# Result blocks of an up stage written to DRAM by GpSimd on its own queue, one tick after they are made, instead of by SyncE two to four ticks after

## The chip, the cores and the metric

One NeuronCore of a Trainium2 chip runs the whole program. The metric is the device time of one execution in microseconds, over several runs; a profiled execution gives the trace. PE is TensorE, DVE is VectorE, ACT is ScalarE, POOL is GpSimd and SP is SyncE, which here only issues transfers.

## The reference

Attention over 4 batches, 12 heads, 448 positions and 64 channels, with q and k normalised, is followed by two feed-forward layers on 1792 tokens of 768 channels, all in float32:

```python
x = attn(rmsnorm(q, g_q), rmsnorm(k, g_k), v)      # -> (1792, 768)
h = maximum(x @ w_in, 0);  x = (h * h) @ w_out      # first layer, 2048 wide
g = x @ w_gate;  val = x @ w_val                    # second layer, 1536 wide
out = (g * sigmoid(g) * val) @ w_out2
```

## The kernel before

The program runs in five stages: attention, then `up(0)`, `down(0)`, `up(1)`, `down(1)`. By the trace they begin at about 0, 252, 458, 670 and 982 us.

Every matrix product of the four last stages is done on 2x2 blocks with seven products P1 to P7 in place of eight. Each float32 operand is split into a high and a low part, and three matmuls (high by high, high by low, low by high) stand for one product. A step of an up stage is nine matmuls of 128x448 on one PSUM bank (L1135). A step of a down stage is eighteen (L1324).

The operands that a down stage multiplies are the four blocks of the up result, B11, B12, B21 and B22, and the sums T1 to T4, which DVE makes of them (`sum_of`, recorded as L1097). They don't fit in the chip's memory together, so each of them except B12 is written to a DRAM tile `hid` by `send` (L1056): 7 names, 2 halves `tp` of the tokens, 8 column groups `g` in the first layer and 6 in the second, 196 transfers of 128x448 floats (224 KB).

Results and sums lie in 16 to 24 `slot`s of the tile `xacc`. A slot is taken from the front of the list `free` and goes to its end when its last reader in program order has been issued (`drop`), the send included. Two landing places for weights lie in the same tile, and a third is taken from slots 3 to 6 when all four are free at once (`claim_third`).

A down stage reads its operands back. `stage` (L1269, `dn<-hid`, 448 KB) fills one of three buffers, `cleave` makes the high part on ACT (L1282) and the low part on DVE (L1097, `xab<-dn` or `xat<-dn`), and PE takes them two steps later. `bring` (L380, `dn<-wkeep`) fetches the weights of the stage. Finished products leave PSUM by L1348 to L1351 into slots.

The order of instructions on every engine is written out by hand by one clock: `clock["n"]` goes on by 1 for each step of an up stage and by 2 for each step of a down stage. One tick is about 1.8 us. A result is put on `sends_due` with a due tick, and `run_sends`, once a step, issues what is due:

```python
if name != "B12":
    sends_due.append((now + 2, (ph, g, tp, name)))
...
    sends_due.append((t + 3 + end, (ph, g, tp, new)))   # end: last group
```

In the kernel before, all transfers of these four stages are issued by SP, in one queue, so that a send waiting for its result holds up the weights and the staged blocks behind it.

Of the kernel before, what the change touches and what calls it, by code (L numbers as in the profile page):

```python
# [19 lines left out]
def kernel(  # L20
# [14 lines left out]
    nc = tc.nc  # L35
# [33 lines left out]
    clock = {"n": 0}  # L69
    state = {"turn": 1, "used": 0, "debt": 0.0, "down": -1, "step": -1, "limit": 4, "tick": 0, "third": False}  # L70

    def slot(s):
        return xacc[:, s * S:(s + 1) * S]
# [928 lines left out]
    def moe():  # L1002
# [22 lines left out]
        hid = [{}, {}]  # L1025
# [7 lines left out]
        sums_due, sends_due = [], []  # L1033

        def run_sends():
            now = [d for d in sends_due if d[0] <= clock["n"]]
            sends_due[:] = [d for d in sends_due if d[0] > clock["n"]]
            for _, args in now:
                send_part(*args)

# [12 lines left out]
        def send(ph, name, g, tp, s):  # L1053
            if (name, g) not in hid[ph]:
                hid[ph][name, g] = mem["keep"].tile([P, 2, S], F32, tag=f"h{ph}_{name}_{g}", name="hid")
            nc.sync.dma_start(out=hid[ph][name, g][:, tp], in_=slot(s))  # L1056
            whole[ph, name, g] = whole.get((ph, name, g), 0) + 1

        parts = {}
# [15 lines left out]
        def send_part(ph, g, tp, name):  # L1075
            m = parts[ph, g, tp]
            send(ph, name, g, tp, m[name])
            drop(m, name)

        def put(ph, g, tp, ij, s):  # L1080
            name = {(0, 0): "B11", (0, 1): "B12", (1, 0): "B21", (1, 1): "B22"}[ij]
            m = parts.setdefault((ph, g, tp), {
                "at": {}, "left": {"B11": 2, "B21": 2, "B22": 3, "T1": 2, "T2": 2, "T3": 1, "T4": 1}})
            when, now = m["at"], clock["n"]
            m[name], when[name] = s, now
            if name != "B12":
                sends_due.append((now + 2, (ph, g, tp, name)))
            end = g == NF[ph] // 2 - 1
            for new, needs, wait in (("T1", ("B11", "B12"), 1 + end), ("T3", ("B22", "T1"), 2),
                                     ("T2", ("B22", "T1"), 3), ("T4", ("B21", "T2"), 2 - end)):  # L1090
                if new not in when and all(x in when for x in needs):
                    t = when[new] = max(when[x] for x in needs) + wait
                    sums_due.append((t, (ph, g, tp, new)))
                    sends_due.append((t + 3 + end, (ph, g, tp, new)))

        def tt(eng, o, a, b, op=ALU.add):
            eng.tensor_tensor(out=o, in0=a, in1=b, op=op)  # L1097
# [4 lines left out]
        def finish_sum(ph, q_, tp, ij, s):  # L1102
            g = ups[ph][q_][1]
            key = g, tp, ij
            if ph == 0:
                fun(s, slot(s), AF.Relu)
                fun(s, slot(s), AF.Square)
                put(ph, g, tp, ij, s)
            elif ups[ph][q_][0] is w_gate:
                fun(s, slot(s), AF.Silu)  # L1110
                gates[key] = s
            else:
                o = gates.pop(key)
                tt(nc.vector, slot(s), slot(s), slot(o), ALU.mult)
                free.append(o)
                put(ph, g, tp, ij, s)
# [27 lines left out]
        def after(ph, p, q_, tp):  # L1144
# [9 lines left out]
            elif p == "P3":  # L1154
                if not paired:
                    outer(ph, q_, tp, L)
            elif p == "P4":
                s = take()
                key = g, tp, (1, 0)
                if ph == 0:  # L1160
                    fun(s, ps, AF.Relu)
                    fun(s, slot(s), AF.Square)
                    put(ph, g, tp, (1, 0), s)
                elif ups[ph][q_][0] is w_gate:
                    fun(s, ps, AF.Silu)
                    gates[key] = s
                else:
                    o = gates.pop(key)
                    tt(nc.vector, slot(s), ps, slot(o), ALU.mult)
                    free.append(o)  # L1170
                    put(ph, g, tp, (1, 0), s)
                idle_banks.append(L["c1"])
            else:
                s, ij = {"P2": ("P1", (0, 0)), "P7": ("P5", (1, 1))}[p]
                s = L[s]
                tt(nc.vector, slot(s), ps, slot(s))
                later(1, finish_sum, ph, q_, tp, ij, s)
                if p == "P2":
                    idle_banks.append(L["c3"])
# [11 lines left out]
        def step(ph, p, q_, tp, rate, last):  # L1191
            group(ph, p, q_, tp)
            if tp == 1:
                assert at[ph, p, q_] == state["used"]
                state["used"] += 1
            clock["n"] += 1
            run_due()
            run_sends()
            run_lows()
            load_raws()  # L1200
            run_types()
            after(ph, p, q_, tp)
            while drain and drain[0][0] <= clock["n"]:
                drain.pop(0)[1]()
            if last and p == "P4":
                stage(ph, 2 + tp)
            pump(rate)
            run_sums()
            if last and (p, tp) in (("P3", 1), ("P4", 0)):
                early = ("P3", "P4").index(p)  # L1210
                cleave(early, 0)
                if early:
                    cleave(0, 1)
            if last and (p, tp) == ("P4", 1):
                cleave(1, 1)
# [68 lines left out]
        def down(ph):  # L1284
# [19 lines left out]
            for n, (p, g) in enumerate((p, g) for p in DOWN for g in range(ng)):  # L1304
# [3 lines left out]
                if n == ng - 1:  # L1308
                    run_sends()
                    assert not due and not sums_due and not sends_due  # L1310
                    free.clear()
# [26 lines left out]
                if g == ng - 1:  # L1338
# [3 lines left out]
                    for tp in range(2):  # L1342
                        for o in range(KT):
# [14 lines left out]
                            if ph and p in ("P1", "P6", "P7", "P4"):  # L1358
                                i, j = {"P1": (0, 0), "P6": (0, 1), "P7": (1, 1), "P4": (1, 0)}[p]
                                k_, t = i * KT + o, 2 * tp + j  # L1360
                                nc.sync.dma_start(out=out[k_ * P:(k_ + 1) * P, t * S:(t + 1) * S], in_=d)
                bring(ph, n + 8)
                run_sends()
                if ph == 0 and n == 2 * ng:
                    state["limit"] = limits[3]
# [76 lines left out]
```

## Time and profile before

| | |
|---|---|
| median of 3 runs | 1138.66 us |
| the runs | 1133.16, 1138.66, 1143.78 us |
| the profiled execution | 1143.64 us |
| its span, first to last instruction | 1141.8 us |
| PE busy in it | 1124.7 us |
| granted TensorE clock | 1.00 throughout |

The profiled execution is one of the longer ones: it lies 5.0 us above the median, and the runs spread over 10.6 us. Outside the span there are 1.8 us.

### The profile page before, as it was taken

The page shows a single profiled execution, that of the slowest core. Times are in us where ns is not written, and L with a number is a line of the kernel's source. Part 1 is how long each engine was busy: PE and PEld are TensorE (multiplying, and loading weights), DVE is VectorE, ACT ScalarE, POOL GpSimd, SP SyncE. Part 2 cuts the span into 40 slices and gives each one's busy share as a digit, 9 for nine tenths or more (in the row PEclk, how much of TensorE's full clock was granted, in tenths as well). Part 3 has the DMA queues.
Part 4 walks back from the last instruction along what each step waited for, and adds up shares of the span by engine and source line. Part 5 has one row for each costly group of instructions (what it writes and reads, how often), then busy time and mean ns, then how long its engine had stood idle before and what let it go on. Part 6 is the DMA issues. An engine that isn't in the chain of part 4 may idle for free.

```text
span 1141.8 us, 17075 instructions
## 1 busy us (share of the span) xinstructions
PE 1124.7 (99%) x6164; PEld 946.3 (83%) x6164; DVE 872.8 (76%) x1253; ACT 637.0 (56%) x1047; POOL 212.2 (19%) x220
## 2 busy tenths in 40 slices
PE   8999999999999999999999999999999999999998
PEld 5555555559899999899999999999999999989998
DVE  7677888759998886998557778978787795775554
ACT  6787887656866776545544545444443434355332
POOL 5899899841000000000000000000000000000000
PEclk9999999999999999999999999999999999999999
DMA  5444322111888988966443302646464651784553
GB/s 169 122 114 126 102 92 83 47 30 30 256 297 257 305 279 269 366 211 204 157 122 121 113 1 100 227 157 208 135 210 132 211 185 53 241 287 136 179 169 138
DMA packets 116676, 189.60 MB, mean 166 GB/s; under 512 B 13936, under 2 KB 97648, under 8 KB 116592
## 3 DMA queue, kind: packets, MB, share of 16 engines
q1 hardware_dynamic: 116272, 188.52, 51.4%
q8 instruction: 48, 0.79, 0.3%
q14 instruction: 36, 0.29, 0.1%
q10 hardware_dynamic: 320, 0.00, 0.0%
HBM read 129.11 MB, written 59.20 MB: 165 GB/s over the span
## 4 chain that ended last, share of the span: by engine, by line
PE 87%; DVE 5%; DMA 3%; ACT 2%; issue 2%; SPq 1%; POOL 0%; DVEq 0%; POOLq 0%; ACTq 0%
PE ps L1135 40%; PE ps L1324 29%; PE s L789 6%; PE s L774 6%; PE s L745 2%; PE s L713 2%; PE s L810 2%; DVE xacc L1097 1%; PE s L754 1%; ACT xacc L1100 1%; DVE xacc L127 1%; DVE ring L268 1%; DMA raw<-in_k_dram 1%; DMA raw<-in_q_dram 1%; DVE xb L150 1%
## 5 line engine op out<-in xcount | busy, mean ns | idle before, releaser
L1135 PE MATMUL ps<-xb,ring 128*128 128x448 f32 x1080 | 228.7, 367 | 0.3 <-ACT xacc L1100 0.3
L1135 PEld LDWEIGHTS ps<-xb,ring 128*128 128x128 f32 x1080 | 202.7, 188 | 19.9 <-ACT xacc L1100 0.7
L1324 PE MATMUL ps<-xat,ring 128*128 128x448 f32 x1008 | 208.7, 368 | 2.7 <-DVE xat L1097 2.7
L1324 PEld LDWEIGHTS ps<-xat,ring 128*128 128x128 f32 x1008 | 189.1, 188 | 22.1 <-DVE xat L1097 3.4
L1135 PE MATMUL ps<-xat,ring 128*128 128x448 f32 x720 | 157.5, 367 | 0.0
L1324 PE MATMUL ps<-xab,ring 128*128 128x448 f32 x756 | 154.5, 366 | 1.8 <-ACT xacc L1348 1.6
L1324 PEld LDWEIGHTS ps<-xab,ring 128*128 128x128 f32 x756 | 141.6, 188 | 14.5 <-ACT xacc L1348 2.4
L1135 PEld LDWEIGHTS ps<-xat,ring 128*128 128x128 f32 x720 | 135.2, 188 | 12.8
L1100 ACT ACTIVATE xacc<-ps 128x448 f32<-128x448 f32 x148 | 79.3, 543 | 104.0 <-PE ps L1135 92.7
L1097 DVE TENSOR_TENSOR xacc<-ps,xacc 128x448 f32<-128x448 f32 x164 | 100.1, 619 | 37.5 <-PE ps L1135 23.4
L265 DVE SCALAR_TENSOR_TENSOR conv<-xacc,conv 128x768 int32<-128x768 int32 x124 | 119.7, 965 | 3.6
L1100 ACT ACTIVATE xacc<-xacc 128x448 f32<-128x448 f32 x148 | 85.0, 577 | 66.8 <-DVE xacc L1097 64.3
L1135 PE MATMUL ps<-xab,ring 128*128 128x448 f32 x540 | 117.7, 367 | 0.0
L748 DVE TENSOR_REDUCE mxz<-s 112x2 f32<-112x896 f32 x96 | 100.4, 1089 | 19.2 <-PE s L745 19.0
L1135 PEld LDWEIGHTS ps<-xab,ring 128*128 128x128 f32 x540 | 101.3, 188 | 10.3 <-issue 0.7
L1282 ACT CAST xat<-dn 128x896 fp32r<-128x896 f32 x56 | 52.9, 944 | 100.6 <-PE ps L1324 64.1
L268 DVE TENSOR_TENSOR ring<-conv,ring 128x384 fp32r<-128x384 f32 x127 | 70.7, 566 | 43.3 <-ACT ring L513 42.1
L780 POOL TENSOR_TENSOR sg<-p 112x896 f32<-112x896 f32 x46 | 96.8, 2106 | 15.0 <-ACT p L776 15.0
L776 ACT ACTIVATE p<-s 112x896 f32<-112x896 f32 x96 | 87.9, 920 | 20.7 <-PE s L774 16.3
L1097 DVE TENSOR_TENSOR xat<-dn,xat 128x896 fp32r<-128x896 f32 x56 | 60.9, 1088 | 37.8 <-ACT xat L1282 37.7
L1097 DVE TENSOR_TENSOR xacc<-xacc 128x448 f32<-128x448 f32 x148 | 88.1, 618 | 1.2
L1282 ACT CAST xab<-dn 128x896 fp32r<-128x896 f32 x42 | 39.6, 944 | 77.8 <-PE ps L1324 60.4
(97 smaller groups left out, 1361.8 us busy)
## 6 DMA issues: line engine op xcount, KB each, us to landing
hid<-xacc SPq DMA_DIRECT2D x196, 224.0 KB
dn<-hid SPq DMA_DIRECT2D x98, 448.0 KB
xacc<-in_moe_w_out_dram SPq DMA_DIRECT2D x28, 768.0 KB
xacc<-in_moe_w_in_dram SPq DMA_DIRECT2D x16, 768.0 KB
xacc<-in_moe_w_gate_dram SPq DMA_DIRECT2D x12, 768.0 KB
xacc<-in_moe_w_val_dram SPq DMA_DIRECT2D x12, 768.0 KB
wkeep<-conv SPq DMA_DIRECT2D x22, 384.0 KB
dn<-wkeep SPq DMA_DIRECT2D x44, 192.0 KB
```

Of the source, the lines that this page charges most:

```text
L265: nc.vector.scalar_tensor_tensor(out=out, in0=in0, scalar=scalar, in1=out, op0=op, op1=ALU.bitwise_or)
L268: nc.vector.tensor_tensor(out=out, in0=a, in1=b, op=ALU.subtract)
L748: nc.vector.tensor_reduce(out=mxz[:, c, 0:P:D], in_=ps[:CP, :, :S], op=ALU.max, axis=AX.X)
L774: nc.tensor.matmul(ps[:CP, a, :S], lhs, rhs, start=(w == 0), stop=(w == 3))
L776: nc.scalar.activation(out=p, in_=ps[:CP, :, :S], func=AF.Exp)
L780: nc.gpsimd.tensor_tensor(out=sg, in0=p_t[pi, 2 * w], in1=p_t[pi, 2 * w + 1], op=ALU.add)
L789: nc.tensor.matmul(ps[s, :S], v_t[pi][:, a, c * D:(c + 1) * D], p[:, a, :], start=(c == 0), stop=(c == NCH - 1),)
L1097: eng.tensor_tensor(out=o, in0=a, in1=b, op=op)
L1100: nc.scalar.activation(out=slot(s), in_=src, func=func)
L1135: nc.tensor.matmul(ps, w[:, wi, kk * P:(kk + 1) * P], xk[:, xi, kk * S:(kk + 1) * S], start=bool(first and mm == 0), stop=(mm == 3 * KT - ...
L1282: nc.scalar.copy(k[:, 0], src)
L1324: nc.tensor.matmul(ps_of(ps[tp, o]), w[:, wi, o * P:(o + 1) * P], h[:, hi, tp * S:(tp + 1) * S], start=bool(first and m == 0), stop=(g == ...
```

## The change

A send is issued by `nc.gpsimd` instead of `nc.sync`. It becomes due one tick after its result or its sum, where it was two ticks for a result and three for a sum (four in the last group). Since due ticks now come before a sum may have been issued, `run_sends` holds back a send whose source is not yet there. Nothing that is computed changes, and the number and size of the transfers stay.

```diff
         def run_sends():
-            now = [d for d in sends_due if d[0] <= clock["n"]]
-            sends_due[:] = [d for d in sends_due if d[0] > clock["n"]]
+            due_ = lambda d: d[0] <= clock["n"] and d[1][3] in parts[d[1][:3]]
+            now = [d for d in sends_due if due_(d)]
+            sends_due[:] = [d for d in sends_due if not due_(d)]
             for _, args in now:
                 send_part(*args)
...
-            nc.sync.dma_start(out=hid[ph][name, g][:, tp], in_=slot(s))
+            nc.gpsimd.dma_start(out=hid[ph][name, g][:, tp], in_=slot(s))
...
             if name != "B12":
-                sends_due.append((now + 2, (ph, g, tp, name)))
+                sends_due.append((now + 1, (ph, g, tp, name)))
...
-                    sends_due.append((t + 3 + end, (ph, g, tp, new)))
+                    sends_due.append((t + 1, (ph, g, tp, new)))
```

PE keeps its order. Three places show what moves. Line numbers from 1036 on are one higher in the changed kernel.

SP at the start of `down(1)`, where weights (`dn<-wkeep`) and staged blocks (`dn<-hid`) are fetched while the last sums are sent. Before:

```order
L1056 DMA hid<-xacc 128x448
L1269 DMA dn<-hid 128x896
L380 DMA dn<-wkeep 128x384 x2
L1056 DMA hid<-xacc 128x448 x2
L1269 DMA dn<-hid 128x896
L380 DMA dn<-wkeep 128x384 x2
L1056 DMA hid<-xacc 128x448 x4
L1269 DMA dn<-hid 128x896
L380 DMA dn<-wkeep 128x384
L1056 DMA hid<-xacc 128x448
```

The same place of SP in the changed kernel:

```order
L1270 DMA dn<-hid 128x896
L380 DMA dn<-wkeep 128x384 x2
L1270 DMA dn<-hid 128x896
L380 DMA dn<-wkeep 128x384 x2
L1270 DMA dn<-hid 128x896
L380 DMA dn<-wkeep 128x384
```

The eight sends are gone from between the fetches, whose own order is the same.

POOL from the end of attention to the end of the program (L828 and L845 are the last steps of attention). Before:

```order
L845 TENSOR_TENSOR xacc<-xu,rb 128x448
L828 TENSOR_TENSOR sp<-sp 56x16
L845 TENSOR_TENSOR xacc<-xu,rb 128x448 x2
L1435 UNCONDITIONAL_BRANCH
L1435 ISA
```

The same place of POOL in the changed kernel:

```order
L845 TENSOR_TENSOR xacc<-xu,rb 128x448
L828 TENSOR_TENSOR sp<-sp 56x16
L845 TENSOR_TENSOR xacc<-xu,rb 128x448 x2
L1057 DMA hid<-xacc 128x448 x196
L1436 UNCONDITIONAL_BRANCH
L1436 ISA
```

All 196 sends stand behind POOL's last arithmetic, with nothing between or behind them.

DVE late in `up(0)`, where weights are converted (L294, L265 into a `conv` buffer) between sums (L1097) and low parts of weight blocks (L268 into a `ring` buffer). Before:

```order
L294 TENSOR_SCALAR conv_78<-conv_78 128x768
L1097 TENSOR_TENSOR xacc<-xacc 128x448
L265 SCALAR_TENSOR_TENSOR conv_78<-xacc,conv_78 128x768
L1097 TENSOR_TENSOR xacc<-xacc 128x448
L268 TENSOR_TENSOR ring_85<-conv_79,ring_85 128x384
L265 SCALAR_TENSOR_TENSOR conv_78<-xacc,conv_78 128x768
L1097 TENSOR_TENSOR xacc<-xacc 128x448
L268 TENSOR_TENSOR conv_79<-conv_79 128x384
L1097 TENSOR_TENSOR xacc<-xacc 128x448 x2
L268 TENSOR_TENSOR ring_86<-conv_80,ring_86 128x384
```

The same place of DVE in the changed kernel:

```order
L268 TENSOR_TENSOR ring_85<-conv_79,ring_85 128x384
L1098 TENSOR_TENSOR xacc<-xacc 128x448
L268 TENSOR_TENSOR conv_79<-conv_79 128x384
L1098 TENSOR_TENSOR xacc<-xacc 128x448 x2
L268 TENSOR_TENSOR ring_86<-conv_80,ring_86 128x384
L294 TENSOR_SCALAR conv_78<-conv_78 128x768
L265 SCALAR_TENSOR_TENSOR conv_78<-xacc,conv_78 128x768 x2
```

The conversion into `conv_78` moves behind two ring blocks, and the one into `conv_77` just ahead of it moves likewise. With slots freed at other ticks, slots 3 to 6 are free together at tick 195 and not at 181, so that five weight loads use two landing places for longer and are issued 2 to 5 ticks later. These two conversions are the only difference on DVE, and ACT has the same two moves.

## Rows read from the trace of the kernel before

**Rows 1.** The page: busy time of an engine, share of the span, instructions.

```profile
PE 1124.7 (99%) x6164; PEld 946.3 (83%) x6164; DVE 872.8 (76%) x1253; ACT 637.0 (56%) x1047; POOL 212.2 (19%) x220
```

**Rows 2.** What PE waited for from 300 to 1020: total us, times, longest.

```profile
PE ps L1324 <- DVE xat L1097: 2.7, 2, 1.6
PE ps L1324 <- ACT xacc L1348: 1.6, 2, 1.3
PE ps L1135 <- ACT xacc L1100: 0.3, 1, 0.3
```

**Rows 3.** Windows: length, busy PE, PEld, DVE, ACT, POOL (instructions); clock, DMA share, GB/s.

```profile
460.00:480.00 20.00, 17.34 (x84) 15.36 (x83) 19.43 (x30) 11.63 (x18) 0.00 (x0) 1.00 1.00 363
480.00:500.00 20.00, 20.00 (x99) 18.16 (x98) 19.65 (x30) 12.06 (x20) 0.00 (x0) 1.00 0.84 297
...
1000.00:1020.00 20.00, 18.21 (x87) 15.67 (x86) 13.53 (x22) 10.82 (x18) 0.00 (x0) 1.00 0.92 326
1020.00:1040.00 20.00, 20.00 (x100) 18.53 (x100) 15.42 (x24) 9.74 (x17) 0.00 (x0) 1.00 0.53 155
```

**Rows 4.** Timeline of PE at 1005: start, us, line, tile, count [idle before <- releaser].

```profile
1007.38 1.49 PE L1324 MATMUL ps<-xab,ring 128*128 128x448 f32 x6 [1.31 <-ACT xacc L1348]
1009.18 7.17 PE L1324 MATMUL ps<-xab,ring 128*128 128x448 f32 x34 [0.32 <-ACT xacc L1348]
```

**Rows 5.** Timeline of ACT in the same place.

```profile
1005.96 0.94 ACT L1282 CAST xab<-dn 128x896 fp32r<-128x896 f32 x1 [1.93 <-DMA dn<-hid]
1006.80 0.96 ACT L1348 COPY xacc<-ps 128x448 f32<-128x448 f32 x2
1008.60 1.98 ACT L1348 COPY xacc<-ps 128x448 f32<-128x448 f32 x4 [0.83 <-DMA hid<-xacc]
```

**Rows 6.** Timeline of SP's queue ahead of it: the issues, with the time until done.

```profile
998.67 0.95 SPq L1056 DMA_DIRECT2D hid<-xacc  x2
999.71 0.44 SPq L1269 DMA_DIRECT2D dn<-hid  x1
...
1002.59 1.91 SPq L1056 DMA_DIRECT2D hid<-xacc  x4
```

**Rows 7.** Timeline of DVE: the four sums that are sent from 1002.59 on.

```profile
991.22 2.22 DVE L1097 TENSOR_TENSOR xacc<-xacc 128x448 f32<-128x448 f32 x4
```

**Rows 8.** Timeline of DVE ahead of PE's waits at 471 and 476.

```profile
470.19 1.08 DVE L1097 TENSOR_TENSOR xat<-dn,xat 128x896 fp32r<-128x896 f32 x1
...
475.14 1.08 DVE L1097 TENSOR_TENSOR xat<-dn,xat 128x896 fp32r<-128x896 f32 x1
```

**Rows 9.** Timeline of PE from 308 to 320: steps of nine matmuls.

```profile
308.20 2.02 PE L1135 MATMUL ps<-xat,ring 128*128 128x448 f32 x9
310.06 2.02 PE L1135 MATMUL ps<-xb,ring 128*128 128x448 f32 x9
...
316.12 1.99 PE L1135 MATMUL ps<-xab,ring 128*128 128x448 f32 x9
317.94 1.99 PE L1135 MATMUL ps<-xb,ring 128*128 128x448 f32 x9
```

**Rows 10.** DVE by shape, 0 to 240: busy us, mean ns | idle before.

```profile
L294 DVE TENSOR_SCALAR conv<-conv 128x768 int32<-128x768 int32 x4 | 2.5, 617 | 0.5 <-ACT conv L292 0.5
...
L268 DVE TENSOR_TENSOR ring<-conv,ring 128x384 fp32r<-128x384 f32 x2 | 1.9, 971 | 0.0
```

**Rows 11.** The same shapes on DVE from 260 to 480.

```profile
L268 DVE TENSOR_TENSOR ring<-conv,ring 128x384 fp32r<-128x384 f32 x44 | 24.7, 573 | 6.9 <-ACT ring L513 5.8 <-PE ps L1135 1.0
L294 DVE TENSOR_SCALAR conv<-conv 128x768 int32<-128x768 int32 x22 | 12.2, 555 | 5.7 <-ACT conv L292 5.6
```

**Rows 12.** A send's issue on SP (ns min/median/max).

```profile
L1056 SPq DMA_DIRECT2D hid<-xacc x196: 319/360/941, 290.6 to 1006.5; - x196
```

**Rows 13.** POOL's own operations by shape over the span.

```profile
L780 POOL TENSOR_TENSOR sg<-p 112x896 f32<-112x896 f32 x46 | 96.8, 2106 | 15.0 <-ACT p L776 15.0
...
L845 POOL TENSOR_TENSOR xacc<-xu,rb 128x448 f32<-128x448 f32 x24 | 31.3, 1303 | 25.3 <-DMA rb<-row 24.6
```

## Prediction

> **What bounds the kernel now.** I read the page first. PE is busy for 1124.7 of the span's 1141.8 us [rows 1], so all waiting together is 17 us, and only what is lost after attention can be touched, since no send is issued before 290 us [rows 12]. The list of what PE waited for from 300 to 1020 comes next [rows 2]: 2.7 us for DVE and 1.6 us for ACT at the two starts of a down stage, and 0.3 us for ACT early in `up(0)`. That is 4.6 us, nearly all there is, and the most that any better order of sends can give back as waiting time: 0.4% of 1143.64. A gain of over 1% (about what a measurement of this kernel can tell from no change, 11.4 us) can't come from waits.
>
> The windows tell which engine is late at these two places [rows 3]. From 460 to 500 DVE is busy for 39.1 of 40 us. From 1000 to 1020 it is not (13.5 of 20), and the DMA engines move 326 GB/s at a share of 0.92. So the first place is DVE's, the second one belongs to the transfers.
>
> The timelines show the second place from the end backwards. PE stands for 1.31 us at 1007.38 and 0.32 us at 1009.18, both times for ACT's emptying of a PSUM bank, L1348 [rows 4]. ACT's first L1348 starts at 1006.80, right behind its cast of a staged block at 1005.96, which had waited 1.93 us for `dn<-hid`; its third one waits 0.83 us for a send that has still to read the slot it writes [rows 5]. The fetch of that staged block was issued by SP at 999.71, behind two sends of 224 KB at 998.67, and four more sends left from 1002.59 on [rows 6]. The sums in those four were made by DVE between 991.22 and 993.44 [rows 7]: they lay ready for some 9 us.
>
> The first place is another matter. PE's two waits there end with a low part on DVE that starts at 470.19 and at 475.14 [rows 8]. DVE works through its list with hardly a gap there [rows 3], and the change leaves that list as it is.
>
> **A second thing that the windows show** is PE's pace. With no wait at all, nine matmuls take 1.86 us from start to start at 308 and 1.82 us at 316 [rows 9], and PE's weight loads fill 18.16 of 20 us in the windows from 480 to 980 (25 of them, one shown) but 18.53 from 1020 to 1120 (5 of them, one shown) [rows 3]; 18.53 stands also in the seven from 320 to 460. The pace changes only at PE's waits: at 312 it goes to the quick one, at 471 to 476 to the slow one, at 1004 to 1009 back to the quick one, each time with a granted clock of 1.00. 18.53 / 18.16 is 2.0%. Over the 528 us from 476 to 1004 the slow pace costs 528 x 0.020 = 10.5 us; over the 159 us ahead of it 3.2 us, over the 131 us behind it 2.7 us. The three runs fit that: 1143.64 - 10.5 = 1133.1 with the middle quick (a run took 1133.16), 1133.1 + 3.2 + 2.7 = 1139.0 with the middle quick and both ends slow (1138.66), and the profiled case itself (1143.78). That the pace of a stretch is drawn anew at each wait is my inference; the spread of 10.6 us over three runs is not.
>
> **The change part by part.** *196 sends leave SP.* Each took some 0.36 us of its queue [rows 12], and more where it stood waiting for its result. At 998 SP is freed of 0.95 us, and the fetch of 999.71 no longer has two sends ahead of it in its queue: 448 KB at 326 GB/s are 1.4 us. It lands 0.95 to 2.3 us earlier if the sends are through by then. They should be, since their sums end at 993.44 at the latest, 6 us ahead of it. The wait of 1.31 us needs 1.3 us; the bounds are 0 (the sends merely travel beside the fetch) and 1.31. I take 1.31, since the upper half of the arrival's range covers it and ACT has room: it stood ready from 1005.96 - 1.93 = 1004.03 on [rows 5], and PE asks for its bank at 1007.38 - 1.31 = 1006.07 [rows 4].
>
> *Sends one tick after the sum.* The sends at 1002.59 now leave about 9 us earlier and the wait of 0.83 us on ACT has no cause left. That gives 0.32 us on PE, with bounds 0 and 0.32. What could be late next is the low part of a staged block on DVE, which follows ACT's cast and comes earlier with it.
>
> *The first place* keeps its 2.7 us: DVE is the late one, with an unchanged list. The bounds are 0 and 2.7, nearest to 0 because fetches that come earlier don't shorten DVE's work. The 0.3 us at 312 I leave where they are.
>
> *Sends on GpSimd.* No row shows a transfer issued there in this kernel. The nearest rows are SP's 0.36 us per send [rows 12] and GpSimd's own operation on a tile of the same size, 1.30 us [rows 13]. I take 1.3, since a program on GpSimd is nearer to the latter. 196 x 1.3 = 255 us, on an engine that has nothing else to do behind attention, so it costs nothing by itself. What hides it is the spacing: `up(0)` makes 112 sends in 206 us, one in 1.84 us. Beyond 1.84 us each, the sends fall behind (a rival below). A send that waits for its sum holds up only other sends, as no other work stands behind it on POOL. Slots are free earlier in program order, so later writers into them meet fewer open sends.
>
> *Five weight loads 2 to 5 ticks later.* This costs at most 5 x 1.82 = 9.1 us of arrival, once, late in `up(0)`. The loads for column group 6 were issued at ticks 185 and 189 and are now issued at 189 and 192; their first block is wanted by PE at tick 202, and the ring lets it be made from tick 196 on. 7 ticks, some 13 us, are left for a transfer and two conversions. So it costs nothing, and up to a few us if a landing takes over 10 us.
>
> The sum: 1.31 + 0.32 = 1.6 us off, 1143.64 - 1.6 = 1142.0 for a run with the paces of the profiled one. The measured median stood 5.0 us below that run, by the paces. From the median it is 1138.66 - 1.6 = **1137.0 us**.
>
> **The rivals.** *No gain.* If the transfers of both queues simply share full DMA engines, the staged block lands when it did, since the same bytes travel at 0.92 of the share from 1000 on [rows 3]. Then only the 0.32 us goes: 1138.3. For it speaks that GB/s is near its highest there; against it that six sends move out to 989 to 994, ahead of the crowd. The Trainium skill, "DMA: Bandwidth & Descriptors", section "Issuing engines are not separate DMA queues", says that transfers started by SP, ACT or GpSimd run on the same 16 DMA engines, so that issuing from several saves only issue time. By that rule the sum would be this rival's; the trace agrees as far as the full share shows, but the rule leaves aside the time of issue, which the change moves too.
>
> *Slower: GpSimd's work for a send slows DVE.* While GpSimd works in attention, DVE's L294 takes 617 ns and L268 971 ns [rows 10]; without it they take 555 and 573 [rows 11]. So an overlapped microsecond costs DVE 0.10 to 0.41 us. It decides where DVE has no slack: seven windows of 20 us from 300 to 1000 have DVE busy for 19.0 us or more (two shown in [rows 3]). With one send of 0.36 to 1.3 us in 1.84 us these lose 140 / 1.84 x (0.36 x 0.10 to 1.3 x 0.41) = 3 to 41 us of DVE. Blocks made ahead take up a part; at 15 us lost on PE it ends at 1152. It decides for slower by over 1% from a loss of some 13 us on. Against it: both rows stand beside GpSimd arithmetic that reads and writes whole tiles, and a send brings no tile through GpSimd; so I give it 0.08. The Trainium skill, "SBUF — State Buffer", section "Who interferes with whom", says that a DVE operation with two inputs in SBUF contends with GpSimd only when GpSimd reads, and that a DVE copy or tensor_scalar in its two-port mode and a GpSimd operation shut each other out. By that rule L268 would lose nothing and only L294 would pay, which alone (0.10 us in the microsecond) is the 3 to 10 us end of this rival.
>
> *GpSimd too slow per send.* At 2.1 us, its dearest row [rows 13], 112 sends take 235 us in place of 206: the last ones of `up(0)` are 29 us late. PE wants the last B21 block some 26 us into `down(0)`, and slots come back late: 10 to 30 us, about 1157.
>
> **How the numbers follow.** Forecast 0.62 (1137.0), no gain 0.26 (1138.3), slower by DVE 0.08 (1152), GpSimd too slow 0.04 (1157). The paces add a spread to the first two: 1133.1 - 1.6 - 2.7 = 1129 with all stretches quick and the first place's waits gone too, and 1143.64 + 3.2 + 2.7 - 1.6 = 1148 with all slow. The range is 1129 to 1148; it leaves out the last two rivals. Under 1127.3 (1% faster) is below the quickest case: 0.02. Over 1150.0: the last two rivals, less their mild ends, and a mishap: 0.10. Within 1%: 0.88.
>
> **What would show it.** In the trace of after, PE should have no wait for L1348 at the start of `down(1)`, and no ACT or PE wait there for a send. PE's waits at the start of `down(0)` should still end with DVE's low parts. SP's queue should show no waits on L1097 ahead of fetches other than for the three staging buffers. L294 and L268 should keep 555 and 573 ns. The pace, by PEld per window, should explain whatever is left. I am wrong if DVE's rows grow, if POOL's queue shows sends waiting on each other, or if PE waits where it did not.

## The result and the profile after

| | before | after |
|---|---|---|
| median of 20 runs each | 1135.69 us | 1146.89 us |
| lowest and highest run | 1133.16 to 1144.39 us | 1139.90 to 1156.21 us |
| the profiled execution, its span | 1143.64, 1141.8 us | 1144.56, 1142.5 us |
| mean granted clock of it | 1.000 | 0.998 |

After over before is 1.0092, with a 95% interval of 1.0067 to 1.0117. The change makes the kernel slower by 0.7 to 1.2%, where I forecast 1137.0 us, a gain of 0.15%.

The two profiled executions differ by 0.7 us of span only, and they would tell nothing if one compared just these. Stage by stage they differ a lot. Each stage is taken from PE's first matmul of it to the next one's, by PE's timeline:

| stage | before | after | difference |
|---|---|---|---|
| attention | 252.30 | 254.26 | +2.0 |
| `up(0)` | 206.1 | 216.6 | **+10.5** |
| `down(0)` and `up(1)` | 523.7 | 514.0 | **-9.7** |
| `down(1)`, to the last matmul's end | 156.3 | 153.8 | -2.4 |

The middle is the pace, which I come to below. The 2.0 us of attention are not the change's: no send is issued before 292.7 us, and over the thirteen profiled executions of this document attention takes 251.4 to 255.4 us. The first thing is what PE waited for from 300 to 1020 us, in the kernel after; it answers to [rows 2].

```profile
PE ps L1136 <- ACT xacc L1101: 6.7, 3, 3.9
PE ps L1325 <- DVE xat L1098: 2.7, 2, 1.7
PE ps L1136 <- DVE ring L268: 0.4, 1, 0.4
PE ps L1325 <- DVE xab L1098: 0.2, 1, 0.2
```

The waits for L1348 (now L1349) at the start of `down(1)` are gone, as forecast. But an up stage now waits 6.7 us for ACT, where it waited 0.3. What ACT and DVE stood for is in the list of all waits from 240 to 1142, also of after:

```profile
ACT xacc L1101 <- DMA hid<-xacc: 25.9, 8, 7.9
DVE xacc L1098 <- DMA hid<-xacc: 16.1, 6, 5.5
```

The kernel before had 4.9 us in two waits on ACT and no such wait on DVE. So DVE and ACT, before they write a slot, wait for a send that is still reading it. The page says the same in one line, the group of DVE's sums, where the idle time ahead of them was 1.2 us before:

```profile
L1098 DVE TENSOR_TENSOR xacc<-xacc 128x448 f32<-128x448 f32 x148 | 88.1, 619 | 17.0 <-DMA hid<-xacc 16.1
```

The longest wait shows the whole chain. Timelines of POOL, of DVE, of ACT and of PE in the kernel after, 444 to 466 us (start, us, line, tile, count, idle before):

```profile
448.40 2.94 POOL L1057 DMA_DIRECT2D hid<-xacc  x5 [1.33 <-DVE xacc L1098]
456.50 1.14 POOL L1057 DMA_DIRECT2D hid<-xacc  x2 [5.15 <-DVE xacc L1098]
```

```profile
447.38 0.62 DVE L1098 TENSOR_TENSOR xacc<-xacc 128x448 f32<-128x448 f32 x1
...
448.39 1.15 DVE L1098 TENSOR_TENSOR xacc<-xacc 128x448 f32<-128x448 f32 x2
449.46 0.55 DVE L268 TENSOR_TENSOR ring<-conv,ring 128x384 fp32r<-128x384 f32 x1
455.47 1.16 DVE L1098 TENSOR_TENSOR xacc<-xacc 128x448 f32<-128x448 f32 x2 [5.47 <-DMA hid<-xacc]
```

```profile
449.53 0.51 ACT L513 CAST ring<-conv 128x384 fp32r<-128x384 f32 x1
457.91 0.98 ACT L1101 ACTIVATE xacc<-ps 128x448 f32<-128x448 f32 x2 [7.87 <-DMA hid<-xacc]
```

```profile
452.66 1.99 PE L1136 MATMUL ps<-xb,ring 128*128 128x448 f32 x9
458.50 3.44 PE L1136 MATMUL ps<-xat,ring 128*128 128x448 f32 x9 [3.85 <-ACT xacc L1101]
461.78 1.99 PE L1136 MATMUL ps<-xb,ring 128*128 128x448 f32 x9
```

The program's list of slots tells what these are, since the counts of sums and sends agree with it one by one. The sum of 447.38 is T3 of column group 5, first half, in slot 14 (tick 205). The five sends from 448.40 on are its own and four more, T3 of the second half among them. With its send slot 14 goes back to the list, from which it is taken at tick 207 for T2 of the second half. DVE comes to this sum at 450.0, 2 us after it made T3, and stands until 455.47. Slot 12, T3 of the second half, goes the same way at tick 209, and ACT stands until 457.91. PE finds no empty bank and stands for 3.85 us.

A send takes long to finish. The times of the sends on POOL in after (ns min/median/max; the second line from issue to landing, in us):

```profile
L1057 POOL DMA_DIRECT2D hid<-xacc x196: 539/539/720, 292.7 to 998.9; - x196
DMA to landing us min/median/max: 2.2/4.1/7.7
```

GpSimd is done with a send in 0.54 us, but the slot is read for 4.1 us in the median and up to 7.7 us. The Trainium skill, "DMA: Bandwidth & Descriptors", section "Anatomy of one DMA — SWDGE (gpsimd) path", gives a fixed 2.0 us and the bytes at 436 GB/s, an estimate of 2.5 us for 224 KB. The trace's least value, 2.2 us, is near that, its median is not. The long landings go with full DMA engines: of the 196 sends, the 21 between whose issue and landing the DMA share is under 0.6 land in 2.3 us in the median, the 147 with a share of 0.8 or more in 4.7. Windows of 5 us of after show the place of the longest wait (columns as in [rows 3]: at the end the clock, the DMA share and GB/s):

```profile
445.00:450.00 5.00, 5.00 (x26) 4.65 (x25) 5.00 (x9) 3.97 (x9) 2.55 (x5) 1.00 0.95 334
450.00:455.00 5.00, 4.65 (x23) 3.96 (x22) 0.01 (x1) 0.03 (x1) 1.24 (x3) 1.00 1.00 315
455.00:460.00 5.00, 1.50 (x4) 1.37 (x5) 2.85 (x6) 1.38 (x3) 1.62 (x3) 0.81 0.65 254
460.00:465.00 5.00, 5.00 (x22) 4.58 (x22) 2.19 (x4) 3.83 (x7) 1.63 (x3) 0.85 0.29 98
```

The DMA engines are full from 445 to 455 while DVE and ACT stand (0.01 and 0.03 us of work in 5). Behind PE's wait the granted clock is 0.81 and 0.85 of full, a mean of its two levels, 1.2 and 2.4 GHz (PE had stood still for 3.85 us), and nine matmuls take 3.28 us from start to start (458.50 to 461.78) in place of 1.82.

**The account of `up(0)`.** PE's waits there are 7.1 us in place of 0.3: +6.8. The nine matmuls at a low clock cost 1.46 us, nine more at 324 behind another wait 0.4, these at a granted clock of 1.00. The pace, slow over some 102 us in after (326 to 428) and over 60 us in before (252 to 312), gives 0.02 x 42 = 0.8. Together 9.5 of 10.5 us. The last 1.0 us lies in the steps beside the waits, which take 0.1 to 0.3 us more than their idle time and nine matmuls: from 310.91 to 314.33 pass 3.42 us, of which 1.44 are the wait and 1.82 the matmuls.

That wait of 1.44 us, the first of the three, comes without the early reuse of slots too. PE waits 1.3 to 1.4 us at the same place in kernels 2, 5, 6, 9 and 10 below, which all hand out the slots of `up(0)` as the kernel before does, and in each of them PE came there at the quick pace. In before (0.3 us) and in kernel 11 (no wait listed) it came at the slow pace, some 1.1 us later. So of the 6.8 us the slots cost some 5.7; the rest goes with the pace.

**The pace** is the one that [rows 9] show. In after it changes at 428, at a gap of 0.15 us, which PE's timeline shows with the clock at 1.00:

```profile
424.97 2.02 PE L1136 MATMUL ps<-xab,ring 128*128 128x448 f32 x9
426.83 2.02 PE L1136 MATMUL ps<-xb,ring 128*128 128x448 f32 x9
428.84 2.09 PE L1136 MATMUL ps<-xat,ring 128*128 128x448 f32 x9
430.78 1.98 PE L1136 MATMUL ps<-xb,ring 128*128 128x448 f32 x9
432.60 1.99 PE L1136 MATMUL ps<-xab,ring 128*128 128x448 f32 x9
```

1.86 us per nine before the gap, 1.82 behind it. In the middle the kernel after was quick all along; its windows there answer to the slow 18.16 of [rows 3], and PE's weight loads are the second pair of numbers:

```profile
500.00:520.00 20.00, 20.00 (x101) 18.54 (x100) 19.22 (x29) 12.40 (x21) 0.00 (x0) 1.00 0.64 204
```

2% of the 494 us from 490 to 984 are 9.9 us, which is the -9.7 of the table. It is the luck of that execution: the lowest runs, 1139.90 and 1133.16, stand 6.7 us apart, and that is near what the traces give when the paces are equal, 5.7 of waits and 1.9 of slower matmuls behind them in `up(0)` less 1.6 in `down(1)`, 6.0 us.

The ratio of 1.0092 is more, 10.5 us. A part of that is the clock: its mean over the 20 runs of after is 0.9968, over the 92 runs of the kernel before in the groups below 0.999, which makes 2.5 us of 1140 in place of the 1.46 of the profiled execution. The other 3 us or so I can't place; only one execution of each kernel has a trace, and the paces of the others aren't known.

### The profile page after: what moved, and what is told of

Its sections match the earlier page's. It is cut to its first block, busy times and chain, and to the rows that moved or that the text cites. A ratio compares the mean times of both kernels' runs of the same rounds, so it can differ in the third digit from the quotient of the medians.

```text
span 1142.5 us, 17159 instructions
## 1 busy us (share of the span) xinstructions
PE 1119.2 (98%) x6164; PEld 947.9 (83%) x6164; DVE 874.2 (77%) x1253; ACT 635.3 (56%) x1047; POOL 322.0 (28%) x416
## 4 chain that ended last, share of the span: by engine, by line
PE 82%; DMA 5%; DVE 4%; issue 4%; ACT 3%; POOL 1%; SPq 0%; POOLq 0%; DVEq 0%; ACTq 0%
PE ps L1136 36%; PE ps L1325 30%; PE s L789 6%; PE s L774 5%; PE s L745 2%; DMA hid<-xacc 2%; PE s L713 2%; PE s L810 2%; DMA dn<-wkeep 1%; ACT xacc L1101 1%; DVE xacc L1098 1%; DVE conv L265 1%; POOL hid L1057 1%; PE s L754 1%; DMA raw<-in_k_dram 1%
## 5 line engine op out<-in xcount | busy, mean ns | idle before, releaser
L1057 POOL DMA_DIRECT2D hid<-xacc x196 | 107.1, 547 | 615.9 <-DVE xacc L1098 530.7
L265 DVE SCALAR_TENSOR_TENSOR conv<-xacc,conv 128x768 int32<-128x768 int32 x124 | 122.8, 990 | 3.7
L268 DVE TENSOR_TENSOR ring<-conv,ring 128x384 fp32r<-128x384 f32 x127 | 69.9, 560 | 38.2 <-ACT ring L513 38.0
```

The source lines that it names most:

```text
L265: nc.vector.scalar_tensor_tensor(out=out, in0=in0, scalar=scalar, in1=out, op0=op, op1=ALU.bitwise_or)
L268: nc.vector.tensor_tensor(out=out, in0=a, in1=b, op=ALU.subtract)
L1057: nc.gpsimd.dma_start(out=hid[ph][name, g][:, tp], in_=slot(s))
```

## The experiments

The theory after this reading (**slots**): what costs is that a slot goes back to the list with its send, one tick after the sum, and is handed out again before the send has read it. The rivals: **the queue** (GpSimd's sends land late or stand behind each other), **the order** (the new order of the sends, or their meeting with weights, makes them land late), and the pace alone. Each ratio is to runs of the kernel before on the same chip. "Lowest" is the lowest of the runs, 12 each if not said otherwise; that of the kernel before was 1131.99 to 1133.16 in every group. The last column is PE's waits for ACT in `up(0)`, in the profiled execution; the 1.3 to 1.4 in it are the wait that goes with the quick pace.

| kernel | median | lowest | ratio [95%] | PE <- ACT |
|---|---|---|---|---|
| after (20 runs) | 1146.89 | 1139.90 | 1.0092 [1.0067, 1.0117] | 6.7 |
| 1 SP, new ticks (6 runs) | 1148.53 | 1147.24 | 1.0121 [1.0085, 1.0157] | 4.8 |
| 2 GpSimd, old ticks | 1137.04 | 1132.94 | 1.0029 [0.9992, 1.0067] | 1.4 |
| 3 T3 alone late (11 runs) | 1143.11 | 1140.79 | 1.0064 [1.0032, 1.0095] | 5.3 |
| 4 slots aged | 1144.90 | 1137.28 | 1.0059 [1.0024, 1.0093] | 5.0 |
| 5 new ticks, old free | 1135.19 | 1132.50 | 0.9979 [0.9940, 1.0018] | 1.4 |
| 6 second layer alone | 1133.71 | 1130.71 | 0.9953 [0.9911, 0.9994] | 1.3 |
| 7 first layer alone | 1148.12 | 1143.39 | 1.0083 [1.0047, 1.0119] | 7.0 |
| 8 sums at two ticks | 1140.90 | 1139.57 | 1.0005 [0.9973, 1.0038] | 7.9 |
| 9 first layer with old free | 1133.80 | 1131.68 | 0.9974 [0.9945, 1.0002] | 1.4 |
| 10 second layer alone, on SP | 1138.68 | 1134.80 | 1.0019 [0.9988, 1.0050] | 1.3 |
| 11 as 6, again | 1134.15 | 1131.09 | 0.9981 [0.9952, 1.0010] | none |

**1 and 2. The queue or the ticks.** One kernel has the new ticks on the old queue, the other one the new queue with the old ticks.

```diff
-            nc.gpsimd.dma_start(out=hid[ph][name, g][:, tp], in_=slot(s))
+            nc.sync.dma_start(out=hid[ph][name, g][:, tp], in_=slot(s))     # 1
```

```diff
-            nc.sync.dma_start(out=hid[ph][name, g][:, tp], in_=slot(s))
+            nc.gpsimd.dma_start(out=hid[ph][name, g][:, tp], in_=slot(s))   # 2, from the kernel before
```

> Sends one tick after their source, as in the changed kernel, but issued by SP in its one queue. Slot theory (with the new ticks a T3 sum's slot goes back to the free list one tick after the sum and is handed out again one tick later, before its send has landed, so that DVE and ACT stand in up(0)): the slots are handed out exactly as in the changed kernel, so it is as slow, about 1146, with waits of DVE and ACT for sends of over 20 us in all and PE waits in up(0) of some 7 us. Queue theory (a send from GpSimd lands later or takes the transfers' bandwidth from others): back near the kernel before, about 1136.

> Sends issued by GpSimd in their own queue, but in program order two to four ticks after their source, as before; slots are handed out exactly as in the kernel before. Slot theory: none of the waits of up(0), PE's waits for L1348 at the start of down(1) gone, about 1134 to 1136. Queue theory: about 1146, with long waits of ACT and DVE for sends all the same.

The new ticks alone cost as much as the whole change, on SP too (1.0121), and with the old ticks on GpSimd no change is measured (1.0029, lowest 1132.94). Both expectations have misses. With the new ticks on SP, ACT and DVE wait 12.8 us for sends and not over 20, and PE 4.8 us in `up(0)` and not some 7; a granted clock of 0.50 from 325 to 330 adds to its loss. GpSimd with the old ticks shows no gain in time, though the waits for L1348 are gone. PE's waits from 300 us on with the new ticks on SP, and all of PE's waits on `ps` from 250 us on with the old ticks on GpSimd:

```profile
PE ps L1136 <- ACT xacc L1101: 4.8, 3, 4.0
...
PE ps L1325 <- ACT xacc L1349: 1.8, 1, 1.8
```

```profile
PE ps L1324 <- DVE xat L1097: 3.6, 3, 2.0
PE ps L1135 <- ACT xacc L1100: 1.4, 1, 1.4
```

The wait at the start of `down(1)` is there as long as the sends are on SP, and gone with GpSimd at either ticks. So the queue doesn't cause the loss, and the ticks do.

**3 and 4. Which slots.** Two kernels try to keep the early sends and spare the reused slots: one sends T3 alone at the old tick, since T3's slots were the ones that came back soonest (of the six slots that are handed out again at two ticks in after, five; in before there is one such slot); the other one hands out a slot only when its result is four ticks old, as far as there is one.

```diff
-                    sends_due.append((t + 1, (ph, g, tp, new)))
+                    sends_due.append((t + (3 + end if new == "T3" else 1), (ph, g, tp, new)))   # 3
```

```diff
+            born[m[name]] = clock["n"]                                      # 4
...
+            born[s] = now
...
-            return free.pop(0)
+            old = [n for n, x in enumerate(free) if born.get(x, -9) + 4 <= clock["n"]]
+            return free.pop(old[0] if old else 0)
```

> The changed kernel with one part undone: the send of T3 alone is due three ticks after its sum (four in the last group) again. Slots are then no longer handed out two ticks after a T3 sum (six times in the changed kernel, once here and before). Slot theory: most of the loss is gone, 1134 to 1138. Queue theory: only one send in seven moves, so it stays at about 1145.

> The changed kernel, but a slot is taken from the free list only when its contents were made at least four ticks ago, where there is such a one. No slot is then handed out under four ticks after it was made. Slot theory: the waits of ACT and DVE for sends in up(0) go, 1133 to 1137. Queue theory: about 1146. Landing places for weights are taken at another tick (161) as a side effect, so that weights come a few ticks earlier.

Both expectations were missed. With T3 late the wait near 455 is gone, but there is one of 5.26 us at 317, with a still lower mean clock behind it, in PE's timeline and in the windows of that kernel:

```profile
317.68 6.67 PE L1136 MATMUL ps<-xb,ring 128*128 128x448 f32 x18 [5.26 <-ACT xacc L1101]
```

```profile
315.00:320.00 5.00, 2.32 (x6) 2.11 (x7) 2.97 (x5) 2.92 (x7) 3.92 (x8) 0.69 0.99 375
320.00:325.00 5.00, 5.00 (x18) 4.47 (x18) 4.90 (x9) 2.46 (x5) 1.19 (x2) 0.63 0.87 245
```

So "T3's slots, reused too early" fell as the whole story. The send that ACT waits for there is that of T3 itself (column group 0, first half, slot 11): the sum at tick 145, the send at 148, the slot handed out at 149. T3's send now stands in the queue behind that of T2, which waits for a later sum until 310.63 us; it is issued at 312.85 and lands at 317.00, and ACT starts at 317.08. So the place of a send in the queue counts too: four ticks were too few for a send that left late. The second kernel missed for another reason: with other slots in use the third landing place was claimed at tick 161 in place of 181, so that the up stage had four slots fewer for longer. ACT's waits for sends rose to 33.7 us in 16. It confounds two things and decides nothing.

**5. The slots alone.** The cleanest cut: all sends as in the changed kernel, but a slot goes back to the list at the tick of the kernel before. The list of slots is then that of before. With it the third landing place for weights is claimed at tick 181 again, so the five weight loads too are where they were; nothing else of the change is undone.

```diff
         def send_part(ph, g, tp, name):
...
-            drop(m, name)
+            m["sent"].add(name)
...
                 sends_due.append((now + 1, (ph, g, tp, name)))
+                drops_due.append((now + 2, m, name))
...
                     sends_due.append((t + 1, (ph, g, tp, new)))
+                    drops_due.append((t + 3 + end, m, new))
```

> The changed kernel with its sends (GpSimd, new ticks, in its order), but a slot goes back to the free list only at the tick of the kernel before. The list of slots handed out is then the same, entry for entry, as in the kernel before. Slot theory: 1134 to 1137, PE waits in up(0) under 2 us. Order theory (not the slots but the new order of sends in the queue makes them land late): it stays at 1143 or more, as with T3 alone held back.

The loss is gone: 0.9979, lowest run 1132.50. PE's waits from 300 on, and those for sends, in this kernel:

```profile
PE ps L1332 <- DVE xat L1105: 2.4, 2, 2.0
PE ps L1143 <- ACT xacc L1108: 1.4, 1, 1.4
```

```profile
ACT xacc L1108 <- DMA hid<-xacc: 16.2, 7, 3.6
DVE xacc L1105 <- DMA hid<-xacc: 6.5, 3, 2.2
```

ACT and DVE still wait for sends, 22.7 us in all, but none of these waits is over 3.6 us, and PE stands for 1.4 us at most on their account. Its waits at the start of `down(1)` are gone. This shows the slots as the cause, against the queue and the order of sends, which are both as in the changed kernel. Against the late weight loads stand kernels 3 and 8: there the third landing place is claimed at ticks 182 and 175, near the 181 of before and not at 195, and the waits of `up(0)` are there all the same.

**6, 7 and 8. Which layer, and how much.** The whole change in one layer alone, and the sums' sends at two ticks in place of one.

```diff
-            nc.gpsimd.dma_start(out=hid[ph][name, g][:, tp], in_=slot(s))
+            (nc.gpsimd if ph else nc.sync).dma_start(out=hid[ph][name, g][:, tp], in_=slot(s))   # 6; 7: the reverse
...
-                sends_due.append((now + 1, (ph, g, tp, name)))
+                sends_due.append((now + (1 if ph else 2), (ph, g, tp, name)))
...
-                    sends_due.append((t + 1, (ph, g, tp, new)))
+                    sends_due.append((t + (1 if ph else 3 + end), (ph, g, tp, new)))
```

```diff
-                    sends_due.append((t + 1, (ph, g, tp, new)))
+                    sends_due.append((t + 2, (ph, g, tp, new)))            # 8
```

> The change made in up(1) and down(1) alone; the first layer is as before. No slot is reused within three ticks of being made there. Slot theory: no loss, and the waits for L1348 at the start of down(1) gone: 1133 to 1136. If sends on GpSimd or the new ticks cost something everywhere: half of the loss, about 1141.

> The change made in up(0) and down(0) alone; the second layer is as before. Slot theory: all six early reuses of T3's slots are here, so it is as slow as the changed kernel or slower by the 1.6 us that down(1) gives: 1145 to 1149. If it costs something everywhere: about 1141.

> The changed kernel with the sends of the sums due two ticks after the sum in place of one. T3's slots are then handed out again three ticks after the sum (six times) where it was two. Slot theory: between the changed kernel and the kernel before, 1138 to 1143, since a tick is 1.8 us and a send from GpSimd took 4.1 us to land. Order theory: near the changed kernel, 1145.

The loss is all in the first layer (1.0083), and the gain, as far as there is one, in the second (0.9953, with an interval that barely leaves out 1). In the first-layer kernel PE's waits are the known ones, and those at `down(1)` stay:

```profile
PE ps L1136 <- ACT xacc L1101: 7.0, 3, 3.9
...
PE ps L1325 <- ACT xacc L1349: 1.6, 2, 1.2
```

At two ticks the median, 1140.90, is where the slot theory had it, and the ratio is 1.0005, which looks harmless; the lowest run, 1139.57, and PE's waits of 7.9 us in the profile don't. Its 12 runs lie within 4.6 us, while the 35 of the kernel before in that group spread from 1131.99 to 1147.79 with a median of 1139.23: the two medians hold different shares of the paces. What this kernel spares is the clock, which is 1.00 all through, beside four waits of at most 3.1 us.

**9, 10 and 11. The way out.** The whole change with the old free ticks in the first layer alone; the second layer alone with its sends on SP; and kernel 6 again.

```diff
-                drops_due.append((now + 2, m, name))
+                drops_due.append((now + (1 if ph else 2), m, name))        # 9, from 5
-                    drops_due.append((t + 3 + end, m, new))
+                    drops_due.append((t + (1 if ph else 3 + end), m, new))
```

```diff
-            (nc.gpsimd if ph else nc.sync).dma_start(out=hid[ph][name, g][:, tp], in_=slot(s))
+            nc.sync.dma_start(out=hid[ph][name, g][:, tp], in_=slot(s))    # 10, from 6
```

> The whole change, but in the first layer a slot goes back to the free list at the tick at which it did before; in the second layer it goes back with its send, as in the changed kernel. So the slots are those of the kernel with the change in the second layer alone (1133.71), and all 196 sends are on GpSimd one tick after their results. Slots theory: 1132 to 1137, ratio 0.993 to 1.000; PE waits in up(0) at most 2 us, no wait for L1349's successor at the start of down(1). Rival (the early sends of the first layer cost something besides the slots): 1138 to 1142, ratio over 1.000, with new PE waits in up(0).

> The first layer as before; in the second layer the sends stay on SP but become due at the new ticks. If the time of the send alone removes the waits at the start of down(1): as with GpSimd, ratio 0.993 to 0.999, no PE wait for L1349 there. If the queue is needed (sends stand ahead of the staged blocks in SP's queue): PE waits 0.5 to 2 us for L1349 there and the ratio is 0.998 to 1.003.

> The kernel with the change in the second layer alone, on another set of runs. Its ratio was 0.9953 [0.9911, 0.9994]. If the gain is the 1.6 us of PE's waits at the start of down(1) alone, the ratio is 0.997 to 1.000; if the first result was right in size, 0.993 to 0.997. A ratio over 1.001 would mean that the first result was the chance of PE's paces.

Number 10 separates what the second layer gains by. PE's timeline and SP's queue of that kernel (sends and fetches side by side) at the start of `down(1)`, and ACT's; the last row is the cast at the same place in kernel 11, which differs by the queue alone:

```profile
999.12 4.13 PE L1325 MATMUL ps<-xab,ring 128*128 128x448 f32 x19 [2.81 <-ACT xacc L1349]
```

```profile
987.83 1.19 SPq L380 DMA_DIRECT2D dn<-wkeep  x2
989.12 2.62 SPq L1057 DMA_DIRECT2D hid<-xacc  x4
991.83 0.73 SPq L1270 DMA_DIRECT2D dn<-hid  x1
```

```profile
997.70 0.94 ACT L1283 CAST xab<-dn 128x896 fp32r<-128x896 f32 x1 [3.70 <-DMA dn<-hid]
998.54 2.70 ACT L1349 COPY xacc<-ps 128x448 f32<-128x448 f32 x6
```

```profile
995.40 0.94 ACT L1283 CAST xab<-dn 128x896 fp32r<-128x896 f32 x1 [0.80 <-DMA dn<-hid]
```

Here the four sends are due earlier, but SP's queue still has them ahead of a fetch of a staged block, and ACT's cast waits 3.70 us for such a block, in kernel 11 0.80. PE's wait of 2.81 us is longer than the 0.5 to 2 expected. So the early ticks bring nothing by themselves in the second layer (1.0019); the waits go with the queue. With GpSimd the wait is gone in kernels 2, 5, 6, 9 and 11. What that is worth in time is less sure. Of the last four of these the ratios are 0.9979, 0.9953, 0.9974 and 0.9981, by their intervals' weights 0.9974 together, some 3 us; they share runs of the kernel before two and two, so I give no interval for that. Of the four intervals one leaves out 1, that of kernel 6, and barely. The sum of the prediction gave 1.6 us, and the lowest runs of 6, 9 and 11 are 1.3 to 2.1 us under that of the kernel before in their groups, while that of 5 is 0.5 us over it. Kernel 2, with the same waits gone, has 1.0029. The repeat, kernel 11, fell where the 1.6 us alone would put it (0.997 to 1.000), and not where a gain of the size of kernel 6 would.

## Why the prediction was wrong

The step that failed is the last sentence on the sends on GpSimd: "Slots are free earlier in program order, so later writers into them meet fewer open sends." They meet more. An earlier tick frees the slot earlier in the program's order, and the list hands it out by that order; whether the send has landed is settled by time. The sends moved by one to three ticks, some 2 to 5 us, but the landing needs 2.2 to 7.7 us whichever tick it is. A writer that came two ticks after the sum was on DVE 2 us behind it. The old three ticks were the slack that hid the landing. I had read them as delay only, though [rows 5] show an ACT write that waits 0.83 us for a send, at old ticks. Kernel 5 shows it: old slots with new sends are 0.9979, and kernel 1 shows a loss of that size without GpSimd.

I priced the step at nothing and gave it no rival. The rows of before don't hold the price: 224 KB at the 363 GB/s of [rows 3] are 0.63 us, far less than two ticks of 1.82 us [rows 9], and no row of before times a send to its landing. But the 0.83 us of [rows 5] show that a send can be late at the old ticks, and that called for a rival with a range and not for nothing. The cost on PE was 6.8 us of waits, some 5.7 of them by the slots, 1.5 us of lower clock and 0.4 us of slow matmuls at full clock, in a stage where PE had waited 0.3 us. Two of the signs of being wrong that I had named came: PE waits where it did not, and POOL stands twice, for 2.7 us in all, for earlier sends.

The other steps:

- *The fetch at `down(1)`* (1.31 us) and *the sends one tick after the sum* (0.32 us): both waits of PE went. That the reason is the queue holds for the first one: kernels 1 and 10, with the new ticks on SP, keep a wait of 1.8 and 2.8 us, and kernel 2, with the old ticks on GpSimd, has none. In kernel 2 the 0.32 us are gone too, so the queue is enough for them; the tick, which I gave the credit, isn't needed.
- *The first place* kept its 2.7 us, and still ends with a low part on DVE. The 0.3 us at 312, which I left where they were, became 1.44 by the quick pace ahead of them.
- *Sends on GpSimd* take 0.55 us, not 1.3, between the bounds of 0.36 and 1.3. Two rivals fall with it. "GpSimd too slow" needed over 1.84 us. "GpSimd's work slows DVE" is met by DVE's rows of after from 260 to 480, which answer to [rows 11]:

```profile
L268 DVE TENSOR_TENSOR ring<-conv,ring 128x384 fp32r<-128x384 f32 x44 | 24.8, 574 | 5.2 <-ACT ring L513 5.1
L294 DVE TENSOR_SCALAR conv<-conv 128x768 int32<-128x768 int32 x22 | 12.3, 560 | 4.7 <-ACT conv L292 4.6
```

  574 and 560 ns against 573 and 555.
- *No gain* is not what happened at `down(1)`: the waits did go. How much time went with them the kernel with that part alone leaves open (0.9953 and 0.9981).
- *The five weight loads* were costed at nothing; no kernel tries them alone. In kernels 3 and 8 the third landing place is claimed near its old tick and the waits of `up(0)` are there, and no wait of PE in after names weights but one of 0.4 us for a ring block at 319.
- *The paces* were right as a spread: a slow stretch of over 50 us is in six of the thirteen traces (before, after, 4, 5, 7 and 11), and the range reached 1148 by them. But they also hid the loss, since 1146.89 lies inside the range by luck: it is another case than the one forecast.

## What to carry to other kernels

A buffer that a transfer reads is free when the transfer has landed, not when it is issued. Where a list hands buffers out in program order, moving the issue forward moves the reuse forward too, while the landing keeps its length; keep the tick of reuse when you move the tick of issue. Count how many ticks old a buffer is when it is handed out, before and after an edit, look at what stands ahead of its transfer in the queue, and set both against the transfer's landing under load.

Sends that stand ahead of late fetches in one queue can hold up the engine that the fetches feed, and a queue of their own took these waits away here. Price that by the wait: here it was 1.6 us of 1140, too little for these runs to tell from nothing.

When one kernel's runs spread by 1%, compare the lowest runs and the stages of the traces beside the medians: two profiled runs with spans of 1141.8 and 1142.5 us hid a stage that was 10.5 us longer.

## What the runs showed of the hardware

- PE has two paces at a granted clock of 1.00, 1.82 and 1.86 us for nine matmuls of 128x448, and holds one for up to 500 us. Mostly it changes at a gap in PE's work; one of 0.15 us at 428 was enough. Not every gap changes it: around the wait of 3.85 us at 458 it is the quick one on both sides. And in kernel 5 it went from slow to quick at 984.8 us, at the first matmul of `down(1)`, with no idle time of PE. Nothing here shows what chooses.
- The granted clock fell at some of PE's waits and not at others. Beside those of 3.85 us (after), 5.26 us (kernel 3) and 4.0 us (kernel 1) windows of 5 us have means of 0.81 and 0.85, of 0.69 and 0.63, and of 0.50, that is, 1.2 GHz for a part or the whole of them. Beside four waits of up to 3.1 us in kernel 8 and one of 2.81 us in kernel 10 it stayed at 1.00. But beside shorter ones, 1.8 to 2.0 us at the start of `down(0)` in kernels 5, 9 and 10, one window each has 0.70, 0.79 and 0.70. So the length of a wait alone doesn't tell. Nine matmuls took 3.28 us from start to start behind the first.
- A send issued on GpSimd occupies it for 0.54 us, against a median of 0.36 us on SP [rows 12], and costs DVE nothing that these rows show. It lands 2.2 us after its issue at the least and 4.1 us in the median, for 224 KB.
